# Sliding-window attention and a squared-ReLU FFN in one program: score bursts of three half blocks, one pool of PSUM banks, and another order of the first tasks

## The chip, the cores and the metric

The kernel runs on one core of one Trainium2 chip. The metric is the device time of one execution in microseconds. The engines are named as in the profile: PE is TensorE, PEld its weight loads, DVE is VectorE, ACT is ScalarE, POOL is GpSimd, SP is SyncE. PE writes to PSUM, which has eight banks of 128 rows by 512 fp32 values; ACT and DVE empty them.

## The reference

What is computed, cut to what matters:

```python
# q, k, v: batch 8, 8 heads, 576 tokens, 64 values a head
scores = q @ k.transpose(0, 1, 3, 2) / 8
rel = pos[:, None] - pos[None, :]
slopes = 2.0 ** (-8.0 * (np.arange(8) + 1) / 8)
mask = (rel >= 0) & (rel < 128)
scores = np.where(mask, scores - slopes[:, None, None] * np.abs(rel), -1e9)
attn = softmax(scores)                       # over the keys
x = (attn @ v).transpose(0, 2, 1, 3).reshape(4608, 512)
h = x @ w_in                                 # 512 x 2048
out = (np.maximum(h, 0.0) ** 2) @ w_out      # 2048 x 512, result 4608 x 512 fp32
```

## The kernel before

**Attention.** Each sequence of 576 tokens is cut into blocks of 128, 128, 128, 128 and 64 tokens, 40 blocks in all (`m` counts them, `NKB` is 5). A query block meets at most two key blocks, the previous one (part 0) and its own (part 1). For each block the kernel

- loads k, q and v with a cast to bf16 from POOL's queue (`load_block`, L356). Block 0 alone gets k and q as fp32 by SP's queue (L348);
- transposes k and q to `kqT`: on PE through PSUM (L425, for block 0 L408) with copies on DVE (L373) and ACT (L375) for the blocks in `KQ_PE`, by a DMA transpose on SP's queue (L398) for the others;
- computes scores in a burst (`score`, L469). A contraction over 64 values uses half of the array's rows, so two heads are multiplied side by side, and the two halves write to different PSUM banks. One burst takes four banks for the eight heads. The 64-token last block of a sequence and the first block of the next one share a burst (`pair`);
- exponentiates each bank on ACT into `P` (L488) and multiplies by a mask on DVE (L496), which holds the window and exp(-slope x distance). `masks` are built on ACT (L273) from `dist` (iota on POOL, L245, then DVE); `pair_masks` are copies of them for pair bursts (L280, L283);
- multiplies P with v and a column of ones (`mix`, L516), takes reciprocals (L539) and normalizes (L544) into `x`, which is transposed into `xT` on PE (L562) for the blocks in `X_PE`, or by a DMA transpose on SP's queue (L554).

**FFN.** Tokens go in nine groups of 512. `fc_step` (L604) multiplies w_in with `xT` into a PSUM bank, ACT applies ReLU (L613), DVE squares (L620). `t_part` (L665) multiplies a tile of 128 tokens with w_out, a quarter of the 16 chunks at a time, all into one bank; ACT copies it out (L636) and SP stores it (L644). `SPLIT` cuts the token ranges of the first two groups finer, since their tokens become available bit by bit. w_in and w_out are loaded in four quarters each (L324, L331). `FIRST` gives the order of the first loads on POOL: b is a block (k, q, v), i a quarter of w_in, o one of w_out.

**What sets the order.** Every operation is a `Task` with the engines that it may run on, an assumed duration, a key (its due time) and the slots that it takes and gives back. `Plan.order` walks through time and gives each engine the task that can start first, the smaller key deciding between equals; the program is then emitted in that order, and on the chip each engine runs its instructions strictly in it. Keys come from `where` (blocks, shifted by `AHEAD`) and from the loop over the groups. The planner knows rings of buffers (`size`: 8 slots for k and q, 8 for v, 5 for `kqT`, 2 for `P`, 4 for `x`) and two pools of PSUM banks (`BANKS`): four banks A, used by score bursts and later attention work, and four banks B, used by the FFN and by the first sequence's transposes and PV products. At most eight transfers of a queue are in flight, so a ninth waits for the first to land. `BEGIN` and `COLD` are assumptions on when POOL starts and until when PE runs at half pace. `fill` puts matmuls with zeros (L705, L707; `WARM` of them at the beginning, L311) where the planner sees PE idle before 26 us.

## Time and profile before

| what | value |
|---|---|
| median of 5 runs | 312.88 us (312.34 to 313.34) |
| the profiled execution's own time | 312.67 us |
| its span, first to last instruction | 310.9 us |
| granted clock of TensorE | 1.00 |
| busy: PE, ACT, DVE, POOL | 302.8, 179.2, 164.8, 107.3 us |
| first FFN matmul | 15.92 us |
| last matmul of the FFN ends | 308.0 us |

Times inside the profile count from the span's first instruction. The span is the time of one execution on the chip from the first to the last instruction; what lies around it, 1.8 us here, is in the measured time only. "Busy" for PE is the union of its matmuls' times; they overlap, so the pace of matmuls is read from one start to the next. In lists of groups and in the order in time, `out<-in` names what is written and read, `xN` is a count, and what stands in brackets or behind a bar is the engine's idle time before the group and what ended it. A few per cent of the matmul records can be missing from a trace, and a gap of one matmul's length is then no stall.

### The profile page before, as it was taken

What the parts mean: (1) busy time and instruction counts of PE and PEld (TensorE: products, weight loads), DVE (VectorE), ACT (ScalarE), POOL (GpSimd) and SP (SyncE); (2) the same over time, 40 slices, a digit from 0 to 9 for tenths busy, and PEclk for the clock granted to TensorE, in tenths of its full rate; (3) what the DMA queues carried; (4) which work ended last, traced back from release to release, by engine and by line L of the source; (5) the groups of instructions that cost most, each with busy time, mean ns of one, the idle gap of its engine ahead of it and who ended that gap; (6) DMA issues with size and microseconds to landing.
All of it is one profiled execution on the core that took longest, in us unless ns stands there. A gap on an engine that the chain in (4) does not pass through costs nothing.

```text
span 310.9 us, 7139 instructions
## 1 busy us (share of the span) xinstructions
PE 302.8 (97%) x2784; PEld 173.7 (56%) x2824; DVE 164.8 (53%) x482; ACT 179.2 (58%) x342; POOL 107.3 (35%) x134
## 2 busy tenths in 40 slices
PE   8899999999999999999999999999999999999996
PEld 8799867665455555454454444445444454444443
DVE  5677666566557867675265555556455542222200
ACT  3767748585467847665555656665456654444411
POOL 8936959765654357357432120100000000000100
PEclk9999999999999999999999999999999999999999
DMA  9999999999999999999999994755422120000021
GB/s 136 180 190 180 173 181 131 171 129 142 153 154 145 120 154 163 154 186 172 208 176 161 134 196 118 137 127 104 130 84 84 53 59 34 37 34 35 34 98 73
DMA packets 168114, 39.86 MB, mean 128 GB/s; under 512 B 159440, under 2 KB 163792, under 8 KB 168080
## 3 DMA queue, kind: packets, MB, share of 16 engines
q0 software_dynamic: 114896, 18.88, 87.0%
q1 hardware_dynamic: 53184, 20.52, 34.5%
q8 instruction: 22, 0.36, 0.5%
q14 instruction: 12, 0.10, 0.1%
HBM read 36.70 MB, written 9.44 MB: 148 GB/s over the span
## 4 chain that ended last, share of the span: by engine, by line
PE 95%; ACT 2%; issue 1%; DVE 1%; DVEq 0%
PE B L604 40%; PE B L665 40%; PE A L469 6%; PE A L516 5%; PE A L311 1%; PE B L516 1%; ACT masks L273 1%; PE B L707 1%; ACT kqT L375 1%; PE A L425 1%; PE B L425 0%; DVE kqT L373 0%; PE A L562 0%; PE B L562 0%; ACT P L488 0%
## 5 line engine op out<-in xcount | busy, mean ns | idle before, releaser
L604 PE MATMUL B<-xT,w_in_sb 128*128 128x512 bf16 (+3 forms) x812 | 144.6, 312 | 1.7 <-issue 0.8
L665 PE MATMUL B<-w_out_sb,g 128*128 128x512 bf16 (+2 forms) x572 | 141.5, 373 | 1.3 <-issue 0.5
L613 ACT ACTIVATE rt<-B 128x512 bf16<-128x512 f32 (+2 forms) x152 | 86.6, 584 | 73.4 <-PE B L604 66.1
L620 DVE TENSOR_TENSOR g<-rt 128x512 bf16<-128x512 bf16 (+2 forms) x152 | 61.2, 405 | 73.5 <-ACT rt L613 72.4
L604 PEld LDWEIGHTS <-w_in_sb 128*128 128x128 bf16 x832 | 66.7, 98 | 48.0
L665 PEld LDWEIGHTS <-g 128*128 128x128 bf16 x592 | 54.2, 98 | 55.9
L488 ACT ACTIVATE P<-A 128x512 bf16<-128x512 f32 (+1 forms) x132 | 69.4, 591 | 19.2 <-PE A L469 19.1
L496 DVE TENSOR_TENSOR P<-P,masks 128x512 bf16<-128x512 bf16 (+1 forms) x104 | 42.4, 413 | 25.7 <-ACT P L488 22.3
L356 POOL DMA_DIRECT2D kq<-in_k_dram x39 | 33.0, 847 | 46.5 <-DMA kqT<-kq 34.8
L356 POOL DMA_DIRECT2D vt<-in_v_dram x40 | 34.3, 858 | 39.5 <-PE A L516 33.8
L356 POOL DMA_DIRECT2D kq<-in_q_dram x39 | 33.2, 852 | 11.2 <-DMA vt<-in_v_dram 4.1
L636 ACT ACTIVATE osb<-B 128x512 f32<-128x512 f32 (+1 forms) x36 | 21.6, 600 | 23.9 <-PE B L665 23.9
L516 PEld LDWEIGHTS <-P 128*128 128x128 bf16 x576 | 26.8, 98 | 14.8 <-DVE P L496 0.5
L644 POOL DMA_DIRECT2D out_dram<-osb x3 | 1.7, 563 | 89.5 <-ACT osb L636 89.5
L544 DVE TENSOR_TENSOR x<-A,rec 128x256 bf16<-128x256 f32 (+1 forms) x70 | 28.8, 418 | 1.3
L516 PE MATMUL A<-vt,P 128*128 128x65 bf16 x504 | 25.8, 193 | 0.0
L469 PEld LDWEIGHTS <-kqT 64*128 64x128 bf16 x576 | 14.9, 94 | 13.0 <-issue 12.2
L469 PE MATMUL A<-kqT,kqT 64*128 64x128 bf16 (+1 forms) x256 | 17.9, 212 | 1.0 <-DVE kqT L373 0.8
L469 PE MATMUL A<-kqT 64*128 64x128 bf16 (+1 forms) x320 | 18.4, 211 | 0.0
L539 DVE RECIPROCAL rec<-A 128x4 f32<-128x4 f32 (+1 forms) x70 | 12.1, 179 | 11.7 <-PE A L516 10.8
L496 DVE TENSOR_TENSOR P<-P,pair_masks 128x512 bf16<-128x512 bf16 x28 | 11.7, 420 | 6.7 <-ACT P L488 5.6
L638 DVE COPY osb<-B 128x128 f32<-128x128 f32 x1 | 0.3, 291 | 13.7 <-PE B L665 13.7
(48 smaller groups left out, 80.8 us busy)
## 6 DMA issues: line engine op xcount, KB each, us to landing
out_dram<-osb SPq DMA_DIRECT2D x32, 256.0 KB, 2.3
vt<-in_v_dram POOLq DMA_DIRECT2D x32, 128.0 KB, 7.1
kq<-in_k_dram POOLq DMA_DIRECT2D x31, 128.0 KB, 7.3
kq<-in_q_dram POOLq DMA_DIRECT2D x31, 128.0 KB, 7.7
w_in_sb<-in_moe_w_in_dram POOLq DMA_DIRECT2D x4, 512.0 KB, 9.6
w_out_sb<-in_moe_w_out_dram POOLq DMA_DIRECT2D x4, 512.0 KB, 9.3
out_dram<-osb POOLq DMA_DIRECT2D x3, 256.0 KB, 2.5
kq<-in_k_dram POOLq DMA_DIRECT2D x8, 64.0 KB, 9.4
```

The costliest lines, as they stand in the source:

```text
L356: nc.gpsimd.dma_start(o, src[b, :, kb * 128:kb * 128 + n, :].rearrange("h s d -> s h d"))
L469: nc.tensor.matmul(slot_s[2 * (c // 2) + half].tile.rearrange("p (c x) -> p c x", c=2)[:, c % 2, at:at + w], kqT[sk_of[mk].idx][rows, c, : ...
L488: nc.scalar.activation(Pv(i), view(slot_s[i].tile.rearrange("p (c x) -> p c x", c=2)), AF.Exp, bias=0.0, scale=scale)
L496: nc.vector.tensor_tensor(pt, pt, view(mk), op=ALU.mult)
L516: nc.tensor.matmul(bank(slot_v)[:, hi * (D + 1):(hi + 1) * (D + 1)], Pt[sP.idx][:, place(h)].rearrange("p t q -> p (t q)")[:, at_of[m, par ...
L539: nc.vector.reciprocal(srec.tile[0:n, :], pv[0:n, :, D])
L544: nc.vector.tensor_tensor(xt[sx.idx][0:n, hf * 256:(hf + 1) * 256].rearrange("p (h e) -> p h e", h=4), pv[0:n, :, 0:D], srec.tile[0:n, :]. ...
L604: nc.tensor.matmul(bank(slot)[:, fi * w:(fi + 1) * w], w_in_sb[:, cc, fc * 128:(fc + 1) * 128], xT[:, cc, g * 512 + lo:g * 512 + hi], star ...
L613: nc.scalar.activation(srt.tile[:, 0:cols], slot.tile[:, 0:cols], AF.Relu, bias=0.0, scale=1.0)
L620: nc.vector.tensor_tensor(sg.tile[:, fcs[0]:fcs[-1] + 1, lo:hi], r, r, op=ALU.mult)
L636: nc.scalar.activation(so.tile[:, lo:hi], slot.tile[:, lo:hi], AF.Copy)
L665: nc.tensor.matmul(bank(slot)[:, lo:hi], sg.tile[:, fc, t * 128:(t + 1) * 128], w_out_sb[:, fc, lo:hi], start=fc == 0, stop=fc == FCB - 1)
```

## The change

- Score bursts: `layout` and `score` replace `score`. The four banks of a block's (or a pair's) scores are two units of two banks. From block 5 on, a burst has three units, that is one and a half blocks, in six banks; before that it has two. `P` and `kqT` slots are taken and given back unit by unit.
- PSUM: one pool of eight banks (`BANKS = {"A": 8}`) for everything. `ration` keeps an FFN task from taking a bank when the next burst is near in time and three banks with FFN results are still held.
- First tasks: another `FIRST` order; v of block 0 comes after block 1's k and q (`V0`); iota comes after the first k load; `ident` in bf16 is a task of its own, later; the masks' columns are the other way round (own block first); the pair masks are built after the masking of block 1; `WARM` is 16 instead of 24; other assumed times (`BEGIN`, `COLD`).
- Group 1's tokens are cut in four pieces instead of two (`SPLIT`). In the built program 64 matmuls of 320 columns become 128 of 128 and 64 of 64.
- `KQ_PE`: block 9's k and q are transposed by DMA, block 11's on PE. The rings of k, q and of v have seven slots instead of eight. Other shifts in `AHEAD` and `EARLY`.

The diff, cut to its core:

```diff
-    BEGIN = {"POOL": 1250.0}
-
-    def __init__(self, bufs, pools, cold):
+    BEGIN = {"POOL": 780.0}
+
+    def __init__(self, bufs, pools, cold, share):
         self.tasks = []
         self.bufs = bufs
-        self.pools, self.cold = pools, cold
+        self.pools, self.cold, self.share = pools, cold, share
+        self.bursts = []
...
+    def ration(self, t, at, banks, left, used, free):
+        nxt = next((b for b in self.bursts if b.start is None), None)
+        if nxt is None or left[nxt] or nxt.key >= t.key:
+            return at
+        if nxt.ready > max(at, free["PE"]) + self.share[1]:
+            return at
+        for s in nxt.acq:
+            if s.tag in self.bufs and s.idx is None:
+                u = used[s.tag]
+                if len(u) >= self.bufs[s.tag] and u[-self.bufs[s.tag]].left:
+                    return at
+        mine = [s for s in banks if s is not None and s.ffn]
+        spare = self.share[0] - 1 - sum(1 for s in mine if s.left)
+        if spare < 0:
+            return None
+        ends = sorted((s.freed for s in mine if not s.left), reverse=True)
+        return max(at, ends[spare]) if len(ends) > spare else at
...
                 if s.tag in held:
+                    if s.ffn:
+                        at = self.ration(t, at, held[s.tag], left, used, free)
+                        if at is None:
+                            return None
...
-    FIRST = "b0 b1 b2 i0 i1 i2 b3 i3 o0 b4 b5 o1 b6 b7 o2 o3 b8 b9"
-    SPLIT = {0: [(0, 128), (128, 256), (256, 384), (384, 512)], 1: [(0, 192), (192, 512)]}
-    EARLY = -80
-    AHEAD = {10: -60, 1: 60, 4: 90, 9: -60, 5: -60, 0: -30, 12: 60, 11: 90, 2: 60, 8: 90, 7: 60, 6: 0, 3: -30, 24: 30, 14: 0, 18: 30, 25: 0, 23: 30, 16: -30, 13: 30, 21: 0, 19: -30}
+    FIRST = "b0 b1 i0 b2 i1 b3 i2 o0 b4 i3 b5 o1 b6 o2 b7 o3 b8 b9"
+    SPLIT = {0: [(0, 128), (128, 256), (256, 384), (384, 512)], 1: [(0, 192), (192, 320), (320, 448), (448, 512)]}
+    EARLY = -20
+    AHEAD = {10: -60, 1: 30, 4: 30, 9: -60, 5: 0, 0: 0, 12: 60, 11: 0, 2: 60, 8: 30, 7: 60, 6: 0, 3: 30, 24: -30, 14: -60, 18: 30, 25: 30, 23: 30, 16: -30, 13: 60, 21: 0, 19: 30, 17: 0, 22: 0}
     LEAD = 20
...
-    KQ_PE = [0, 1, 2, 3, 4, 5, 6, 7, 8, 9]
+    KQ_PE = [0, 1, 2, 3, 4, 5, 6, 7, 8, 11]
     X_PE = [0, 1, 2, 3, 4, 5, 7, 8, 12, 17]
-    WARM = 24
+    WARM = 16
     FILL, UNTIL = 0.8, 26e3
-    COLD = 0
-    BANKS = {"A": 4, "B": 4}
+    COLD = 5000
+    QUARTERS = 99
+    V0 = 1
+    SHARE, SOON = 3, 500
+    LONG, UNITS = 5, 3
+    W_IN = [0, 4, 8, 12, 16]
+    PAIR_AFTER, PAIR_KEY = 1, -140
+    BANKS = {"A": 8}
...
-    size = {"kq": 8, "v": 8, "kqT": 5, "P": 2, "x": 4}
+    size = {"kq": 7, "v": 7, "kqT": 5, "P": 2, "x": 4}
...
-        nc.gpsimd.iota(dist, pattern=[[-128, 2], [1, 128]], base=128, channel_multiplier=-1,
+        nc.gpsimd.iota(dist, pattern=[[128, 2], [1, 128]], base=0, channel_multiplier=-1,
                        allow_small_or_imprecise_dtypes=True)
 
-    t_iota = plan.add({"POOL": 360.0}, -9.1e5, build_iota)
+    t_iota = plan.add({"POOL": 360.0}, -9e5 + 1.005, build_iota)
...
-        nc.vector.tensor_single_scalar(ident32, dist[:, 1], 0.0, op=ALU.is_equal)
+        nc.vector.tensor_single_scalar(ident32, dist[:, 0], 0.0, op=ALU.is_equal)
+
+    t_ident = plan.add({"DVE": 480.0}, -9e5 - 1, build_ident, [t_iota])
+
+    def build_ident16():
         nc.vector.tensor_copy(ident, ident32)
 
-    t_ident = plan.add({"DVE": 350.0}, -9e5 - 1, build_ident, [t_iota])
+    t_ident16 = plan.add({"DVE": 230.0}, -9e5 + 1, build_ident16, [t_ident])
...
+    t_pair = [plan.add({"DVE": n}, PAIR_KEY, f, t_mask) for n, f in ((670.0, pair_rest), (960.0, pair_own))]
...
-            t_in[m, nm] = load(key + 0.01 * i, 870.0 * n / 128, emit, deps, [sl])
+            t_in[m, nm] = load(key + 0.01 * i + V0 * (m == 0), 870.0 * n / 128, emit, deps, [sl])
...
+    def layout(ms):
         sP = Slot("P")
-        t_P = []
         pair = len(ms) == 2
-        slot_s = [Slot("A") for _ in range(4)]
         work_of = []
         for i, m in enumerate(ms):
             b, kb, n, _, first = where(m)
             parts_of[m] = ([(0, m - 1)] if kb else []) + [(1, m)]
-            P_of[m] = (sP, t_P)
+            P_of[m] = (sP, [])
             for part, mk in parts_of[m]:
-                at = 128 * i + 64 * part if pair and i == 0 else 128 * part
+                at = 64 * (1 - part) if pair and i == 0 else 128 if pair else 128 * (1 - part)
                 at_of[m, part] = at
                 rel = [sk_of[mk]] if part == 0 or kb == NKB - 1 else []
                 work_of.append((m, mk, n, at, rel))
-        lo = min(w[3] for w in work_of)
-        hi = max(w[3] + w[2] for w in work_of)
-        n = 128 if pair else work_of[0][2]
+        for m in ms:
+            P_of[m] = P_of[ms[0]]
+        return ms, sP, work_of, where(ms[0])[3]
+
+    def score(units):
+        first_of = [u for u in units if u[1] == 0]
+        due = units[0][0][3]
+        slots = {}
+        for (ms, sP, work_of, _), j in units:
+            for half in range(2):
+                slots[ms[0], 2 * j + half] = Slot("A")
 
         def burst():
-
-            for sl in slot_s:
+            for sl in slots.values():
                 bank(sl)
-            for c in range(C):
-                for m, mk, w, at, _ in work_of:
-                    for half in range(2):
-                        rows = slice(half * 64, half * 64 + 64)
-                        nc.tensor.matmul(
-                            slot_s[2 * (c // 2) + half].tile.rearrange("p (c x) -> p c x", c=2)[
-                                :, c % 2, at:at + w],
-                            kqT[sk_of[mk].idx][rows, c, :], kqT[sk_of[m].idx][rows, C + c, 0:w],
-                            start=True, stop=True)
-        tm = plan.add({"PE": 220.0 + C * sum(max(w[2], 64) / 2.4 + 4 for w in work_of)}, due - 28, burst,
-                      [t for w in work_of for x in w[:2] for t in t_kq_of[x]] + chain["s"], slot_s + [sP],
-                      [x for w in work_of for x in w[4]])
+            for (ms, sP, work_of, _), j in units:
+                for c in (2 * j, 2 * j + 1):
+                    for m, mk, w, at, _ in work_of:
+                        for half in range(2):
+                            rows = slice(half * 64, half * 64 + 64)
+                            nc.tensor.matmul(
+                                slots[ms[0], 2 * j + half].tile.rearrange("p (c x) -> p c x", c=2)[:, c % 2, at:at + w],
+                                kqT[sk_of[mk].idx][rows, c, :], kqT[sk_of[m].idx][rows, C + c, 0:w],
+                                start=True, stop=True)
+        tm = plan.add({"PE": 220.0 + 2 * sum(max(w[2], 64) / 2.4 + 4 for u in units for w in u[0][2])}, due - 28, burst,
+                      [t for u in units for w in u[0][2] for x in w[:2] for t in t_kq_of[x]] + chain["s"],
+                      [*slots.values()] + [u[0][1] for u in first_of],
+                      [x for u in units if u[1] == 1 for w in u[0][2] for x in w[4]])
+        plan.bursts.append(tm)
         chain["s"] = [tm]
-        for i in range(4):
-            def view(t):
+        for (ms, sP, work_of, due), j in units:
+            pair = len(ms) == 2
+            hi = max(w[3] for w in work_of) // 128 + 1
+            lo = min(w[3] for w in work_of) // 128
+            n = 128 if pair else work_of[0][2]
+            cols = 2 * sum(w[2] for w in work_of)
+
+            def view(t, pair=pair, lo=lo, hi=hi, n=n):
                 if pair:
                     return t
-                return t.rearrange("p c (t q) -> p c t q", t=2)[:, :, lo // 128:2, 0:n]
-
-            def Pv(i=i):
-                return view(Pt[sP.idx][:, 2 * i:2 * i + 2].rearrange("p h t q -> p h (t q)"))
-
-            def expo(i=i):
-                nc.scalar.activation(Pv(i), view(slot_s[i].tile.rearrange("p (c x) -> p c x", c=2)),
-                                     AF.Exp, bias=0.0, scale=scale)
-            cols = 2 * sum(w[2] for w in work_of)
-            te = plan.add({"ACT": act(cols)}, due - 28 + 3 * i, expo, [tm], [], [slot_s[i]])
-
-            def mask(i=i):
-                pt = Pv(i)
-                mk = (pair_masks if pair else masks.rearrange("p h t q -> p h (t q)"))[:, 2 * i:2 * i + 2]
-                nc.vector.tensor_tensor(pt, pt, view(mk), op=ALU.mult)
-            t_P.append(plan.add({"DVE": dve(cols, 2)}, due - 28 + 3 * i, mask,
-                                [te] + (t_pair if pair else [t_mask[h] for h in range(H) if place(h) // 2 == i])))
+                return t.rearrange("p c (t q) -> p c t q", t=2)[:, :, lo:hi, 0:n]
+
+            for i in (2 * j, 2 * j + 1):
+                slot = slots[ms[0], i]
+
+                def Pv(i=i, sP=sP, view=view):
+                    return view(Pt[sP.idx][:, 2 * i:2 * i + 2].rearrange("p h t q -> p h (t q)"))
+
+                def expo(i=i, Pv=Pv, view=view, slot=slot):
+                    nc.scalar.activation(Pv(i), view(slot.tile.rearrange("p (c x) -> p c x", c=2)),
+                                         AF.Exp, bias=0.0, scale=scale)
+                te = plan.add({"ACT": act(cols)}, due - 28 + 3 * i, expo, [tm], [], [slot])
+
+                def mask(i=i, pair=pair, Pv=Pv, view=view):
+                    pt = Pv(i)
+                    mk = (pair_masks if pair else masks.rearrange("p h t q -> p h (t q)"))[:, 2 * i:2 * i + 2]
+                    nc.vector.tensor_tensor(pt, pt, view(mk), op=ALU.mult)
+                P_of[ms[0]][1].append(plan.add(
+                    {"DVE": dve(cols, 2)}, due - 28 + 3 * i, mask,
+                    [te] + (t_pair if pair else [t_mask[h] for h in range(H) if place(h) // 2 == i])))
...
+    units, ready = [], []
     while m < NBLK:
         ms = [m, m + 1] if m % NKB == NKB - 1 and m + 1 < NBLK else [m]
         for x in ms:
             turn(x)
-        score(ms)
-        for x in ms:
-            mix(x)
+        what = layout(ms)
         m += len(ms)
+        for j in range(2):
+            units.append((what, j))
+            if j:
+                ready.append(ms)
+            if len(units) < (UNITS if ms[0] >= LONG else 2) and not (m >= NBLK and j):
+                continue
+            score(units)
+            units = []
+            for done_ms in ready:
+                if done_ms[0] == PAIR_AFTER:
+                    for t in t_pair:
+                        t.deps += P_of[done_ms[0]][1]
+                for x in done_ms:
+                    mix(x)
+            ready = []
...
-        slot = Slot("B")
+        slot = Slot("A")
+        slot.ffn = True
...
```

Other places change `Slot("B")` to `Slot("A")`, set `slot.ffn` for the FFN, and let `SPLIT` pieces wait for their own quarter of w_in.

## The prediction

> **What bounds the kernel now.** I read the page first (busy shares, the chain that ended last), then the order in time on TensorE (PE) and on the other engines for the first 45 us, then the landings of the transfers, last the waits.
>
> The page:
>
> ```profile
> span 310.9 us, 7139 instructions
> PE 302.8 (97%) x2784; PEld 173.7 (56%) x2824; DVE 164.8 (53%) x482; ACT 179.2 (58%) x342; POOL 107.3 (35%) x134
> ...
> PE 95%; ACT 2%; issue 1%; DVE 1%; DVEq 0%
> ```
>
> PE is the bound: 95% of the chain. A busy PE need not be at its peak, so I took the distance from each matmul's start to the next. From the first FFN matmul (15.92) on, every one runs at its form's own pace: 216 ns for 512 columns, 136 for 320, 83 for 192, 56 for 128, 29 for 65. Gaps of one matmul too many are missing records (2784 matmuls against 2824 weight loads: 40). Real stalls are 0.21 us at 24.1, 0.11 at 33.7, 0.09 at 52.1, and none after. So later only the amount of PE work and the cost of changing kinds of work can move the end.
>
> A score burst in the order in time (start, length, engine, line, tiles, count), its middle left out:
>
> ```profile
> 104.17 1.46 PE L604 MATMUL B<-xT,w_in_sb 128*128 128x512 bf16 x6
> 105.56 0.23 PE L469 MATMUL A<-kqT,kqT 64*128 64x128 bf16 x2
> ...
> 105.96 0.22 PE L469 MATMUL A<-kqT 64*128 64x128 bf16 x2
> 106.11 0.39 PE L665 MATMUL B<-w_out_sb,g 128*128 128x512 bf16 x1
> ```
>
> The last of the six starts at 104.17 + 5 x 0.216 = 105.25, the burst 0.31 later instead of 0.216: 95 ns to go over to 64-row matmuls. From the last pair's second matmul to the next full one are 149 ns instead of 53: 96 ns to come back. A burst costs 0.19 us besides its pairs (57 ns each at 128 columns), whatever its length.
>
> The start:
>
> ```profile
> 6.48 0.60 PE L408 MATMUL B<-ident,kq 128*128 128x128 f32 x4
> ...
> 15.92 1.05 PE L604 MATMUL B<-xT,w_in_sb 128*128 128x128 bf16 x16
> ...
> 7.12 0.69 DVE L373 CAST kqT<-B 128x512 bf16<-128x512 f32 x1 [2.07 <-PE B L408]
> ...
> 6.67 2.55 ACT L273 ACTIVATE masks<-dist 128x256 bf16<-128x256 f32 x8
> 9.12 1.18 ACT L488 ACTIVATE P<-A 128x256 bf16<-128x256 f32 x4
> ```
>
> ACT builds the eight masks after its copy of kqT, and exp waits for it. This sets the 15.92. Two issues of loads on POOL, and from the answers for them alone the time to landing (min/median/max):
>
> ```profile
> 12.57 0.80 POOL L324 DMA_DIRECT2D w_in_sb<-in_moe_w_in_dram  x1
> ...
> 20.16 0.68 POOL L356 DMA_DIRECT2D vt<-in_v_dram  x1 [2.11 <-DVE x L544]
> ```
>
> ```profile
> DMA to landing us min/median/max: 6.9/9.6/12.2
> ```
>
> ```profile
> DMA to landing us min/median/max: 9.2/9.2/9.2
> ```
>
> The last quarter of w_in lands at 12.57 + 12.2 = 24.8 and is first read at 26.1; v of block 4 lands at 29.3. The loads land in order, one 128-row block per 0.85 us, one weight quarter per 2.5, without a pause from 12 us: in the first 45 us a load's place in the queue decides its time. Before, the least margin between landing and use there is 1.0 us.
>
> **The change, part by part.**
> *Bursts.* Before: 33 (26 single blocks, 7 pairs). After: 5 of blocks 0 to 5, then 56 half units in threes, 19; 24 in all. Nine times 0.191 = -1.72 us; pairs and columns stay. The Trainium skill (TensorEngine Tiling, Key Properties) says that a change of tiling mode drains TensorE, and TensorE: Matmul & The Clock Gate (Single matmul latency) puts a drain near 175 ns: an estimate of 2 x 175 x 9 = 3.15 us. The rows show 95 and 96 ns; I take 1.72.
> *Group 1's split.* 64 matmuls of 320 columns become 128 of 128 and 64 of 64: 128 x 56 + 64 x 29 (the 65-column pace) - 64 x 136 = +0.32 us.
> *One pool, FFN held.* No operation. A long burst takes six banks and leaves two. The Trainium skill speaks against it (TensorEngine Tiling, Gotcha 1: row tiling raises PSUM pressure; Perfetto Trace Analysis, Optimization Strategy: a bubble that recurs can mean that PSUM ran out). By the rows: exp frees a bank every 0.48 us (four in 2.06), the first 0.8 after the burst; an FFN step of four matmuls fills one per 0.86, a tile of the second GEMM one per 3.5. The two free banks carry PE 1.7 us, by when two exps are done; with a relu (0.49) per step, ACT needs 0.97 against PE's 0.86 for six steps, 0.7 us behind at most, inside that lead. Bounds are that and 0; I take 0; without cover, ACT's lag, up to 0.7, falls on PE at each of 19 bursts. In the new order I counted PE work between each bank's last write and its reuse against ACT's and DVE's queues: least slack after 55 us 0.15 us (before: over 0.3). The same count names before's stalls at 24.1, 33.7 and 52.1.
> *The start.* POOL issues block 1's k and q first (0.86 each), iota between them, then v0, v1 and w_in's first quarter. Iota ends 1 us later, but ident waits for DVE's memsets anyway (to 2.2). Both fp32 copies go to DVE (0.69 each; 7.8 as now). ACT starts the masks at 4.7, when dist is ready, and ends them at 7.1 instead of 9.2. Block 1's q is the fourth transfer instead of the fifth (8.0 before, about 7.2), so its transposes stand ahead of burst 0 at no cost. Burst 1 goes from 11.3 to 8.7; eight exps end at 11.6; mask, norm, four transposes and copy of x follow: first FFN near 13.5, -2.4. The pair masks (0.34 + 0.53 on DVE) move behind block 1's masks, into that chain only ahead of x1.
> *What that meets.* w_in's third quarter now comes after block 3: the same loads as had landed with v3 before (11.70 + 11.1 = 22.8). The fourth comes after w_out's first and block 4: those that had landed with v4 (29.3). I take 0.2 off each for the earlier first issue. PE's work from first FFN to the third quarter: 79 x 56 + 16 x 29 + 16 transposes and 9 fillers x 56 + two bursts (1.3) = 7.6 us plus 0.4 of stalls by my count: there at 21.5, waits to 22.6. Thence 6.5 us more (85 x 56, 3 x 216, 16 x 29, 12 x 56): 29.1; the fourth quarter's landing says 29.2. Of 2.4 us won, some 1.5 go back. What is late next is w_out's second (before 33.7, same place; needed near 35.9): covered.
> *Behind this gate.* From 26.1 to its last matmul at 308.0, PE takes 281.9 us before. After, behind the same first use, by counts: FFN in +100 x 56 + 64 x 29 - 64 x 136 = -1.24; FFN out -3 x 216 = -0.65; 16 PV x 29 = -0.46; 12 transposes x 56 = -0.67; 9 bursts -1.72; a filler -0.06. Sum -4.8: 277.1.
> *Block 9's transpose to DMA, block 11's to PE; rings of 8 to 7; new due times.* PE and ACT work equal. On SP block 9's transpose now stands with block 10's ahead of x of block 6: nothing if that x is written later than both issue, which by order it is. A load has six blocks (some 37 us) of lead against 14.6 at most to land. Three x transposes have 8.6, 9.05 and 9.07 us from issue to use; rows of that stage:
>
> ```profile
> L554 SPq DMA_TRANSPOSE xT<-x x5: 1208/1317/2212, 78.6 to 105.1; - x5
> ...
> DMA to landing us min/median/max: 7.6/8.4/9.2
> ```
>
> They land 0.6 us late to 1.5 early (before, the tightest had 8.64 and 1.05 us to spare). A kqT has 10.7 against 7.6 to 12.1. Bounds 0 to 2 us; taken 0, as before's closest did not stall.
> *Sum.* 29.2 + 277.1 = 306.3 against 308.0; the tail of copy and store (2.9 us) stays. 312.67 - 1.7 = 311.0 for the profiled execution; the median is 0.2 above it: **311.2 us**.
>
> **The rivals.**
> 1. *No gate at the weights.* Loads come 1.2 us sooner than I place them; PE reaches the fourth quarter at 13.5 + 14.1 + 0.4 = 28.0. Then -2.9: 310.0. For it: q3 took 1.44 us instead of 0.85 before, which need not recur. Against: the queue never rests.
> 2. *Late transposes.* One or two x or kqT transposes between 60 and 112 us stop PE by 0.5 to 2 us in all: 311.7 to 313.2. For it: the distances above. Against: the tightest before still had a margin, and smaller rings put fewer loads in front.
> 3. *Bank waits: slower.* PE waits on ACT in or after each of the 19 long bursts. It decides at (1.7 + 0.6) / 19 = 0.12 us each; at 0.25 the time is 311.2 + 4.8 = 316.0, at 0.15 314.0. For it: slacks of 0.15. Against: ACT is 58% busy and banks return faster than FFN takes them.
> That the bursts do not get longer is excluded: the built order has 24.
>
> **How the numbers follow.** Mine 0.50 (310.6 to 311.9), rival 1 0.20, rival 2 0.17, rival 3 0.13. Range 309.8 to 312.9: rival 1 whole, rival 2 nearly, rival 3 out. The measurement tells 0.2% (0.63 us) from no change: faster than 312.25, mine and 1 nearly whole and a third of 2: 0.74; same 0.13 (most of rival 2); slower 0.13 (rival 3).
>
> **What would show it.** Right: 24 bursts at 95 and 96 ns; masks done by 7.5; first FFN at 13 to 14; a stall of some 1 us at w_in's third quarter near 22; no later stall over 0.3. Wrong: waits of PE on ACT at the ends of bursts (rival 3), on xT or kqT (2), none near 22 (1), or a first FFN later than 15.

## The result, and the profile after

The changed kernel takes 311.85 us (median of 26 runs, 311.0 to 313.46) against 312.88 us of the kernel before (47 runs): ratio 0.9974, 95% interval 0.9965 to 0.9982. The forecast was 311.2 us. The direction and the range held, the size did not: of 1.7 us forecast, 1.0 us came by the medians and 0.8 us by the means, which the ratio compares. In 3 of the 26 runs (312.98 to 313.46 us) the mean granted clock was 0.995 instead of 0.999 or more, a clock that no run of the kernel before has on record, and without them the gain is 1.0 us by the means too. The profiled execution took 312.47 us.

The page of the changed kernel:

```profile
span 310.7 us, 7356 instructions
PE 301.9 (97%) x2905; PEld 177.5 (57%) x2945; DVE 161.2 (52%) x475; ACT 179.1 (58%) x336; POOL 107.5 (35%) x134
...
PE 89%; DMA 7%; POOL 2%; issue 1%; DVE 0%; POOLq 0%
```

PE is still the bound, but the chain that ended last now leads through transfers: DMA has 7% of it.

A long burst in the order in time on PE (start, length, engine, line, tiles, count), its middle left out:

```profile
103.94 0.38 PE L729 MATMUL A<-w_out_sb,g 128*128 128x512 bf16 x1
104.25 0.23 PE L507 MATMUL A<-kqT,kqT 64*128 64x128 bf16 x2
...
104.88 0.22 PE L507 MATMUL A<-kqT 64*128 64x128 bf16 x2
105.03 1.04 PE L667 MATMUL A<-xT,w_in_sb 128*128 128x512 bf16 x3
```

The burst starts 0.31 us behind the matmul ahead of it, and the next full matmul 0.15 us behind the last pair: 95 and 96 ns over, as before. There are 24 such bursts instead of 33.

The start, ACT:

```profile
5.12 2.56 ACT L306 ACTIVATE masks<-dist 128x256 bf16<-128x256 f32 x8 [3.10 <-DVE dist L294]
8.91 0.60 ACT L407 ACTIVATE kqT<-A 128x512 bf16<-128x512 bf16 x1 [1.22 <-DVE kqT L405]
9.40 3.17 ACT L536 ACTIVATE P<-A 128x256 bf16<-128x256 f32 x8
13.87 0.60 ACT L407 ACTIVATE xT<-A 128x512 bf16<-128x512 bf16 x1 [1.30 <-PE A L610]
```

DVE's two fp32 copies to kqT:

```profile
6.89 1.47 DVE L405 CAST kqT<-A 128x512 bf16<-128x512 f32 x2 [1.44 <-PE A L440]
```

and PE, with the wait ahead of a group and its releaser in brackets:

```profile
5.87 0.97 PE L440 MATMUL A<-ident,kq 128*128 128x128 f32 x4
7.02 0.61 PE L440 MATMUL A<-ident,kq 128*128 128x128 f32 x4
...
8.51 0.40 PE L507 MATMUL A<-kqT 64*128 64x128 bf16 x8
...
13.45 0.39 PE L610 MATMUL A<-ident,x 128*128 128x128 bf16 x4
13.67 0.33 PE L770 MATMUL A<-ident,zero 128*128 128x128 bf16 x3
14.22 0.40 PE L458 MATMUL A<-ident,kq 128*128 128x128 bf16 x4 [0.22 <-DMA kq<-in_k_dram]
15.28 0.40 PE L458 MATMUL A<-ident,kq 128*128 128x128 bf16 x4 [0.66 <-DMA kq<-in_q_dram]
15.51 0.39 PE L772 MATMUL A<-zero 128*128 128x128 bf16 x4
15.73 0.44 PE L667 MATMUL A<-xT,w_in_sb 128*128 128x128 bf16 x5
```

The masks end at 7.68 instead of 9.2. But the exps do not follow them: ACT stands idle for 1.22 us until DVE has written kqT, makes a copy of its own, and starts the exps at 9.40, later than the 9.12 of the kernel before. x of block 0 is transposed at 13.45 and copied by 14.47. Then the transposes of block 2's k and q stand ahead of the first FFN matmul on PE, and they wait for their loads. The first FFN matmul starts at 15.73, against 15.92 before and 13.5 in the forecast. In the kernel before, the same transposes of block 2 waited for nothing:

```profile
12.34 0.61 PE L425 MATMUL B<-ident,kq 128*128 128x128 bf16 x8
```

Those loads on POOL (block 2's k and q), and from the answer for the two alone the time from issue to landing:

```profile
6.10 0.93 POOL L388 DMA_DIRECT2D kq<-in_k_dram  x1
6.97 0.93 POOL L388 DMA_DIRECT2D kq<-in_q_dram  x1
```

```profile
DMA to landing us min/median/max: 8.1/8.2/8.3
```

They land at 14.2 and 15.2, behind w_in's first quarter. Before, ahead of that quarter in the queue, they landed at 9.7 and 10.6.

The waits of PE from 10 to 35 us, and below them those from 36 us to the end (us in total, times, longest):

```profile
PE A L458 <- DMA kq<-in_q_dram: 0.7, 1, 0.7
PE A L667 <- DMA w_in_sb<-in_moe_w_in_dram: 0.4, 1, 0.4
PE A L507 <- DVE kqT L405: 0.3, 1, 0.3
PE A L458 <- DMA kq<-in_k_dram: 0.2, 1, 0.2
```

```profile
PE A L729 <- issue: 0.6, 4, 0.2
PE A L667 <- issue: 0.5, 3, 0.2
```

All waits lie in the first 35 us. Those called "issue" are gaps of one 512-column matmul, that is, records that the trace lacks. No engine and no transpose holds PE later.

### The profile page after: what moved, and what is told of

It is laid out like the page before. It is cut to its first block, busy times and chain, and to the rows that moved or that the text cites. A ratio compares the mean times of both kernels' runs of the same rounds, so it can differ in the third digit from the quotient of the medians.

```text
span 310.7 us, 7356 instructions
## 1 busy us (share of the span) xinstructions
PE 301.9 (97%) x2905; PEld 177.5 (57%) x2945; DVE 161.2 (52%) x475; ACT 179.1 (58%) x336; POOL 107.5 (35%) x134
## 4 chain that ended last, share of the span: by engine, by line
PE 89%; DMA 7%; POOL 2%; issue 1%; DVE 0%; POOLq 0%
PE A L729 40%; PE A L667 38%; PE A L564 5%; PE A L507 5%; DMA kq<-in_q_dram 4%; DMA vt<-in_v_dram 3%; POOL kq L388 1%; PE A L458 1%; PE A L610 1%; POOL vt L388 1%; POOL w_in_sb L357 0%; POOL dist L274 0%; DVE osb L701 0%; POOLq L274 0%; POOLq L808 0%
## 5 line engine op out<-in xcount | busy, mean ns | idle before, releaser
L667 PE MATMUL A<-xT,w_in_sb 128*128 128x512 bf16 (+3 forms) x944 | 147.9, 293 | 1.6 <-issue 0.5
L729 PE MATMUL A<-w_out_sb,g 128*128 128x512 bf16 (+2 forms) x568 | 143.5, 373 | 1.7 <-issue 0.6
L676 ACT ACTIVATE rt<-A 128x512 bf16<-128x512 f32 (+1 forms) x146 | 85.4, 600 | 73.7 <-PE A L667 59.1
L683 DVE TENSOR_TENSOR g<-rt 128x512 bf16<-128x512 bf16 (+1 forms) x146 | 61.0, 418 | 84.6 <-ACT rt L676 83.7
L667 PEld LDWEIGHTS <-w_in_sb 128*128 128x128 bf16 x960 | 70.9, 98 | 48.2 <-DMA w_in_sb<-in_moe_w_in_dram 0.6
L543 DVE TENSOR_TENSOR P<-P,masks 128x512 bf16<-128x512 bf16 (+1 forms) x104 | 42.4, 411 | 19.9 <-ACT P L536 16.4
L388 POOL DMA_DIRECT2D kq<-in_q_dram x39 | 33.4, 856 | 13.6 <-DMA kq<-in_k_dram 5.8
L699 ACT ACTIVATE osb<-A 128x512 f32<-128x512 f32 (+1 forms) x36 | 21.7, 602 | 22.2 <-PE A L729 21.2
L564 PEld LDWEIGHTS <-P 128*128 128x128 bf16 x576 | 26.3, 98 | 12.7
L592 DVE TENSOR_TENSOR x<-A,rec 128x256 bf16<-128x256 f32 (+1 forms) x80 | 32.3, 414 | 0.6
L564 PE MATMUL A<-vt,P 128*128 128x65 bf16 x576 | 29.2, 193 | 0.0
L587 DVE RECIPROCAL rec<-A 128x4 f32<-128x4 f32 (+1 forms) x80 | 13.6, 176 | 9.5 <-PE A L564 8.2
L543 DVE TENSOR_TENSOR P<-P,pair_masks 128x512 bf16<-128x512 bf16 x28 | 11.6, 419 | 3.3 <-ACT P L536 2.6
L407 ACT ACTIVATE kqT<-A 128x512 bf16<-128x512 bf16 (+1 forms) x9 | 5.2, 580 | 8.5 <-DVE kqT L405 5.8
## 6 DMA issues: line engine op xcount, KB each, us to landing
w_in_sb<-in_moe_w_in_dram POOLq DMA_DIRECT2D x4, 512.0 KB, 10.4
```

Of the source, the lines that this page charges most:

```text
L388: nc.gpsimd.dma_start(o, src[b, :, kb * 128:kb * 128 + n, :].rearrange("h s d -> s h d"))
L543: nc.vector.tensor_tensor(pt, pt, view(mk), op=ALU.mult)
L564: nc.tensor.matmul(bank(slot_v)[:, hi * (D + 1):(hi + 1) * (D + 1)], Pt[sP.idx][:, place(h)].rearrange("p t q -> p (t q)")[:, at_of[m, par ...
L587: nc.vector.reciprocal(srec.tile[0:n, :], pv[0:n, :, D])
L592: nc.vector.tensor_tensor(xt[sx.idx][0:n, hf * 256:(hf + 1) * 256].rearrange("p (h e) -> p h e", h=4), pv[0:n, :, 0:D], srec.tile[0:n, :]. ...
L667: nc.tensor.matmul(bank(slot)[:, fi * w:(fi + 1) * w], w_in_sb[:, cc, fc * 128:(fc + 1) * 128], xT[:, cc, g * 512 + lo:g * 512 + hi], star ...
```

## How the runs are compared

Two times describe each profiled execution: F, the start of the first FFN matmul, and E, the start of PE's last matmul. The whole time is 4.8 to 4.9 us above E in every kernel (312.67 and 307.81 before, 312.47 and 307.61 after). E - F, less the waits of PE that lie between the two, is the PE work; F and those waits tell what the start and the loads do. A ratio below is the mean time of a kernel over the mean time of the kernel before on the same chip; times from different chips differ by some tenths of a us, so that kernels are compared by their ratios.

| kernel | block 2's q lands | F | E | E - F |
|---|---|---|---|---|
| before, three profiles | 10.6, 10.4, 11.3 | 15.92, 16.05, 15.77 | 307.81, 308.08, 307.65 | 291.9, 292.0, 291.9 |
| changed, three profiles | 15.2, 14.6, 15.1 | 15.73, 15.13, 15.59 | 307.61, 307.22, 306.65 | 291.9, 292.1, 291.1 |
| w_in's first quarter behind block 2 | 10.8 | 15.43 | 306.19 | 290.8 |
| before, quarter ahead of block 2 | 14.4 | 18.66 | 310.55 | 291.9 |
| PE's block 2 behind the FFN | 16.3 | 14.69 | 307.83 | 293.1 |
| pause ahead of the quarter, twice | 14.6, 14.5 | 15.09, 14.98 | 306.36, 306.05 | 291.3, 291.1 |
| first quarter in halves | 13.0 | 15.14 | 305.96 | 290.8 |
| halves, block 2's k and q first, twice | 11.1, 11.0 | 14.32, 14.22 | 305.67, 306.30 | 291.4, 292.1 |
| long bursts up to block 19 | 14.9 | 15.35 | 307.86 | 292.5 |
| the load order of before in the changed kernel | 11.9 | 16.47 | 310.01 | 293.5 |
| pause behind the quarter | 14.9 | 15.43 | 307.54 | 292.1 |
| halves with the pause | 13.5 | 15.67 | 307.21 | 291.5 |

## The experiments

**The place of w_in's first quarter.** My first reading was a dry transfer queue: the quarter is the fifth load on POOL now, and the four block loads ahead of it are too few to cover its slow start. Two kernels move only this load on POOL. Four kernels ran on one chip, the changed kernel among them.

> The changed kernel once more, beside the kernel before on the same chip. All theories: 0.2 to 0.4% faster, some 311.9 us; first FFN matmul near 15.7 us, w_in's third quarter landing near 24.5 and its fourth near 30.8.

Measured: 311.73 us, ratio 0.9961 (0.9947 to 0.9976).

```diff
+    done.remove(t_win[0])
+    done.insert(done.index(t_in[2, "v"]) + 1, t_win[0])
```

> The changed kernel with one move on POOL: w_in's first quarter is issued after block 2's three loads instead of ahead of them; no other engine's order changes. Theory (the transfer queue runs nearly dry behind the fifth load, because a weight quarter takes 2 to 4 us from its issue to full rate and four block loads are too few to cover that): every load from block 2's on lands about 1.8 us sooner, k and q of block 2 near 10 us, the third quarter near 22.5, the fourth near 29.2; the first FFN matmul starts near 13.5 to 14.5 unless the first quarter itself is then late; time about 310.3, 0.5% below the changed kernel. Rival (a first weight quarter is slow wherever it stands, so that the loss belongs to the quarter and not to its place): the third and fourth quarters still land near 24.5 and 30.8, time 311.8.

Measured: 311.33 us, ratio 0.9960 (0.9944 to 0.9976), not told apart from the changed kernel. Block 2's q landed at 10.8, but the quarter only at 15.4, and the first FFN matmul waited for it: F 15.43. The third quarter landed at 23.0 and the fourth at 29.8, against 23.6 and 30.3 beside it. The wait for block 2 (0.3 to 1.1 us in the three profiles of the changed kernel) was exchanged for one of 1.0 us for the quarter; PE met none behind it. The expectation named this only as an exception.

In the kernel before, the same move the other way:

```diff
+    done.remove(t_win[0])
+    done.insert(done.index(t_in[1, "v"]) + 1, t_win[0])
```

> The kernel before with one move on POOL: w_in's first quarter is issued after block 1's three loads instead of after block 2's, fifth in the queue as in the changed kernel; no other engine's order changes. Theory of the dry queue: loads from block 2's on land 1 to 2 us later than in the kernel before, w_in's fourth quarter near 26 instead of 24.8; the least margin was 1.0 us there, so PE stops for up to 1 us: 312.9 to 313.9. Rival (the quarter is slow wherever it stands): later loads land as before within 0.3 us and the time is 312.9.

Measured: 315.42 us, ratio 1.0072 (1.0051 to 1.0094). The loads behind block 2 landed within the spread of the kernel before (fourth quarter 25.5), as the rival said. The time went to what both had overlooked: block 2's k landed at 13.6 instead of 9.7, PE waited 2.0 us for it and 0.4 us for q, and then ran at half clock for 3.4 us (see the last section). F rose by 2.7, E - F stayed at 291.9.

Two more profiles of the kernel before:

> The kernel before once more, for a second look at its landings. Theory (up to block 2's v the loads land 4.6 to 5.0 us behind their issue, one per issue on POOL, and only from w_in's first quarter on does the transfer itself set the pace): again 4.6 to 5.0 us for every load up to block 2's v, the first quarter at 14.3 to 14.9, third 19.5 to 20.0, fourth 24.6 to 25.1, block 4's v 29.2 to 29.7. If the landings of single looks differ by 1 us, the lateness seen in the changed kernel may be chance.

Measured: 312.98 us; the first quarter came later than the expected 14.3 to 14.9. Its landing, issued at 7.6, from the answer for this load alone:

```profile
L324 POOL DMA_DIRECT2D w_in_sb<-in_moe_w_in_dram x1: 817/817/817, 7.6 to 7.6; - x1
...
DMA to landing us min/median/max: 8.4/8.4/8.4
```

It landed at 16.0, the fourth quarter at 26.2: both 1.4 us later than in the profile that the forecast was made from, with E only 0.3 later.

> A third look at the landings of the kernel before. The two looks so far have w_in's first quarter at 14.55 and 16.00 us, its fourth at 24.77 and 26.17. Theory (the first weight load takes 3.5 to 3.9 us from the load before it, and 2.8 in the first look was the exception): again 3.5 us or more, first quarter at 15.3 or later, fourth at 25.5 or later, and a time that hardly follows it (312.5 to 313.1), since the kernel before has 1.0 us to spare there. Rival (2.8 is usual, and the changed kernel's order makes the loss): 14.8 or earlier and 25.1 or earlier.

Measured: 312.57 us; quarters at 14.8 and 25.0. So the answer lies between. As the eighth load on POOL the first quarter landed 2.8, 3.7 and 2.3 us behind the load ahead of it in the kernel before, and 3.6 and 3.5 us in two variants of the changed kernel (the one with the quarter behind block 2, and the next one below). As the fifth, with no pause ahead, it took 3.7 to 5.0 us in eight profiles, 4.0 on the mean, and 2.7 in the profile of the changed kernel shown above, where v of block 1 itself came late, at 10.7. The fifth place costs some 0.5 to 1 us there, and single profiles scatter by as much.

**The whole load order of before in the changed kernel**

```diff
-    FIRST = "b0 b1 i0 b2 i1 b3 i2 o0 b4 i3 b5 o1 b6 o2 b7 o3 b8 b9"
+    FIRST = "b0 b1 b2 i0 i1 i2 b3 i3 o0 b4 b5 o1 b6 b7 o2 o3 b8 b9"
-    V0 = 1
+    V0 = 0
```

> The changed kernel with the load order of before (block 2 ahead of w_in, w_in's quarters together, v of block 0 at its old place), the rest kept and planned anew; 24 bursts as in the changed kernel. Theory (bursts give 1.7, group 1's split takes 0.3, and the new load order gains nothing because the fifth load leaves the queue short): 311.3 to 311.9, no more than 0.3 from the changed kernel. Rival (the new load order does give what was forecast for the start): 312.2 or more. Third way (it even costs): 310.9 or less. Fourth quarter near 25.1, first FFN matmul 14.8 to 15.5.

Measured: 314.16 us, ratio 1.0031 (1.0015 to 1.0047). My 311.3 to 311.9 was wrong. The first quarter landed at 16.4, F was 16.47, and PE waited 0.4 and 0.5 us for w_in's second and third quarters and 0.3 for a q at 56 us. With the rest of this plan the new load order is worth some 2 us (0.57% by the ratios); that it gains nothing is refuted. The plan around it was made anew and its due times were not.

**The bursts.** Three kernels go back to one block or pair a burst, from block 5, 14 or 20 on:

```diff
-    LONG, UNITS = 5, 3
+    LONG, UNITS = 5, 2
```

> The changed kernel without the long bursts: every burst is one block or pair (33 instead of 24), the rest of the change kept and planned anew. Theory (a burst costs 0.19 us, six banks held cost nothing): 9 x 0.191 = 1.7 us more than the changed kernel, 313.6. Rival (bank waits after long bursts eat part of the gain): less than 1 us more, 312.0 to 312.8, or none.

```diff
-            if len(units) < (UNITS if ms[0] >= LONG else 2) and not (m >= NBLK and j):
+            if len(units) < (UNITS if LONG <= ms[0] < 14 else 2) and not (m >= NBLK and j):
```

> The changed kernel with long bursts only up to block 13; from block 14 on a burst is one block or pair again: 31 bursts instead of 24, the start untouched. Theory (0.19 us for each burst, bank waits nothing): 7 x 0.191 = 1.3 us slower than the changed kernel, 313.0 to 313.3. Rival (the long bursts' gain is partly eaten by waits): 0.3 to 0.8 us slower, 312.1 to 312.6.

Measured: 317.13 us, ratio 1.0139 (1.0104 to 1.0174), and 318.19 us, ratio 1.0174 (1.0148 to 1.0199): 3.5 and 5 us more than the theory gave. The planner's new order issues transposes by DMA too late. From the waits of PE behind 36 us, first of the kernel with short bursts from block 14, then of the one from block 5:

```profile
PE A L667 <- DMA xT<-x: 2.8, 1, 2.8
```

```profile
PE A L507 <- DMA kqT<-kq: 3.0, 3, 2.1
```

In the first of the two the xT in question was issued at 106.76 and landed 7.6 us later, no slower than the 7.2 to 9.6 of the changed kernel, but PE wanted it at 111.9. This is what the second rival of the forecast described, in a neighbour of the kernel. For the bursts these two runs say nothing; block 20 lies behind that stretch:

```diff
-            if len(units) < (UNITS if ms[0] >= LONG else 2) and not (m >= NBLK and j):
+            if len(units) < (UNITS if LONG <= ms[0] < 20 else 2) and not (m >= NBLK and j):
```

> The changed kernel with long bursts up to block 19 and single blocks or pairs from block 20 on: 29 bursts instead of 24. The order of all work up to about 165 us is that of the changed kernel, so that the stretch from 60 to 115 us, where the kernels with short bursts from block 5 and from block 14 stopped for transposes by DMA, is untouched. Theory (0.19 us for each burst, bank waits nothing): 5 x 0.191 = 0.95 us above the changed kernel, 312.8, with no stall of PE after 35 us. Rival (long bursts' gain partly eaten by waits for banks): 0.2 to 0.6 us above. Third way (any new order brings late transposes): 2 us or more above, with the stall to be seen.

Measured: 313.04 us, ratio 1.0004 (0.9989 to 1.0018) against 0.9974 of the changed kernel: 0.30% or 0.94 us for five bursts, with no wait behind 36 us. The two intervals leave some 0.5 us either way, but E - F less waits says the same: 292.05 against 290.8 to 291.4. 0.19 us for a burst holds.

**The early wait or the row of loads?** One kernel delays the loads, one takes the early wait away on PE alone. In the first, POOL does three more iotas ahead of the quarter:

```diff
         for t in done:
+            if t is t_win[0]:
+                for _ in range(3):
+                    nc.gpsimd.iota(idle, pattern=[[128, 2], [1, 128]], base=0, channel_multiplier=-1,
+                                   allow_small_or_imprecise_dtypes=True)
             t.emit()
```

> The changed kernel with three more iotas into an unused tile on POOL, 1.0 us in all, ahead of w_in's first quarter; the order of all else as it was. Theory (the landings of block 2's k and q and of w_in's quarters set the end one for one): every load from w_in's first quarter on lands 0.8 to 1.0 us later and the time rises by as much, to 312.6 to 312.8; if the longer wait at block 2's k lowers the granted clock, as in the kernel before with its first quarter moved ahead, up to 1.5 more. Rival (PE is not held by the landings, the missing gain lies elsewhere): 311.6 to 312.0.

Measured: 311.30 us, ratio 0.9945 (0.9932 to 0.9959). Wrong in sign: the quarter, issued 1.2 us later, landed at 12.0 instead of the 12.7 to 13.6 of the eight profiles with the same order of loads and no pause ahead. So the run was repeated with the changed kernel and two variants on one chip.

> The changed kernel once more, on the chip of its variants: 311.7 to 311.9 by all theories, first FFN 15.1 to 15.7, stalls at w_in's third quarter and block 4's q of 0.5 to 1.2 us in all.

Measured: 312.05 us, ratio 0.9987 (0.9970 to 1.0003), 0.15 us above the expected range.

> The three iotas ahead of w_in's first quarter once more. If the 311.30 of the first time is real: again 0.3 to 0.6 us below the changed kernel, with the first quarter landing near 12 us although issued 1.2 us later, and block 2's q and all later loads no later than in the changed kernel. If it was chance: 311.7 or more.

Measured: 311.18 us, ratio 0.9955 (0.9939 to 0.9971). The gain came twice: 0.29% and 0.32% by the ratios, against the changed kernel's first runs and against those beside it. POOL in that kernel, the landing of the quarter, and what the transfers moved in single microseconds (busy times of PE, PEld, DVE, ACT and POOL with their counts, then clock, transfer share and GB/s):

```profile
5.37 1.24 POOL L796 IOTA idle<- 128x256 f32 x3
6.55 0.77 POOL L358 DMA_DIRECT2D w_in_sb<-in_moe_w_in_dram  x1
```

```profile
DMA to landing us min/median/max: 5.5/5.5/5.5
```

```profile
8.00:9.00 1.00, 0.68 (x18) 0.60 (x18) 0.06 (x2) 0.96 (x3) 1.00 (x2) 1.00 0.73 40
9.00:10.00 1.00, 1.00 (x28) 0.90 (x23) 1.00 (x5) 1.00 (x4) 1.00 (x3) 1.00 1.13 185
10.00:11.00 1.00, 1.00 (x22) 0.97 (x20) 0.89 (x5) 1.00 (x3) 1.00 (x2) 1.00 1.22 197
```

The same for the changed kernel beside it:

```profile
8.00:9.00 1.00, 0.94 (x18) 0.65 (x15) 0.49 (x2) 0.39 (x1) 1.00 (x2) 1.00 1.11 133
9.00:10.00 1.00, 0.74 (x20) 0.63 (x20) 0.48 (x2) 1.00 (x5) 1.00 (x2) 1.00 1.06 158
10.00:11.00 1.00, 1.00 (x24) 0.98 (x22) 0.90 (x5) 1.00 (x4) 1.00 (x2) 1.00 1.27 185
```

With the pause the transfers nearly stop at 8 to 9 us and the quarter then starts at once at 185 GB/s; without it, it comes to 185 only at 10 to 11 us. A dry queue costs nothing here, so my first theory falls. To see which neighbours slow the quarter, the pause went behind it:

```diff
-            if t is t_win[0]:
+            if t is t_in[2, "k"]:
```

> The changed kernel with the three iotas (1.0 us) behind w_in's first quarter and ahead of block 2's k on POOL. Theory A (the quarter is slowed by the loads that are issued behind it while it runs): it lands near 11 us, 5.5 behind its issue at 5.35, block 2's q near 14.5 to 14.8, time 311.0 to 311.4. Theory B (the quarter is slowed by the four block loads ahead of it, and a pause there lets them drain): it lands at 12.7 to 13.3 as in the changed kernel, block 2's q at 14.7 to 15.5 or later, time 311.7 to 312.1.

Measured: 311.91 us, ratio 0.9976 (0.9963 to 0.9989); the quarter landed at 13.2, block 2's q at 14.9. This is theory B: it is what stands ahead of the quarter that matters, not what follows. Why block loads in front slow it is not settled.

Now the early wait, taken away by the order of tasks (indices into the emitted list):

```diff
+    part = done[117:168]
+    turn_2 = [part[i - 117] for i in (117, 118, 120, 121, 122, 123, 124, 125, 126, 128, 132)]
+    burst_2 = [part[i - 117] for i in (145, 153, 163)]
+    rest = [t for t in part if t not in turn_2 + burst_2]
+    cut = rest.index(done[157])
+    done[117:168] = rest[:cut] + turn_2 + rest[cut:] + burst_2
```

> The changed kernel with block 2's eight transposes, their two copies and its burst moved behind the first 16 to 26 FFN matmuls on PE, ACT and DVE; the loads are as they were. The first FFN matmul then waits only for x and w_in's first quarter and starts near 14.0 instead of 15.1 to 15.7 us. Theory (the wait for block 2's q is where the forecast start failed, and the end follows it): up to 1.1 us less than the changed kernel, 310.7 to 311.2, with small stalls later. Rival (the landings of w_in's third quarter near 23.5, block 4's q near 27.5 and the fourth quarter near 30 hold PE anyway): the stalls there grow by what is won before, and the time stays within 0.4 us of the changed kernel, 311.4 to 311.9.

Measured: 312.10 us, ratio 0.9976 (0.9962 to 0.9990), level with the 312.05 beside it. F came to 14.69, but:

```profile
14.69 0.44 PE L667 MATMUL A<-xT,w_in_sb 128*128 128x128 bf16 x5 [0.46 <-ACT xT L407]
...
19.74 0.90 PE L667 MATMUL A<-xT,w_in_sb 128*128 128x128 bf16 x13 [0.76 <-DMA w_in_sb<-in_moe_w_in_dram]
```

What is won at block 2's q is lost again: 0.76 us at w_in's second quarter (landed at 19.7 in this profile, where all loads from the first quarter on were late; 18.0 to 18.6 in the three of the changed kernel), and 0.59 us at block 2's own burst, for a kqT that the move made late. The median of 12 runs, which does not hang on one profile, shows no gain either. So the time is as the rival said: taking away this one wait gains nothing. That the row of loads sets the pace is what this profile and the swap suggest; the second wait of 0.59 us is a cost of the move itself and has nothing to do with loads.

**Smaller first pieces.** So a version must move the loads. The first quarter in two halves, the second behind block 2:

```diff
-    FIRST = "b0 b1 i0 b2 i1 b3 i2 o0 b4 i3 b5 o1 b6 o2 b7 o3 b8 b9"
+    FIRST = "b0 b1 i0 b2 i1 i2 b3 i3 o0 b4 i4 b5 o1 b6 o2 b7 o3 b8 b9"
-    W_IN = [0, 4, 8, 12, 16]
+    W_IN = [0, 2, 4, 8, 12, 16]
```

> The changed kernel with w_in's first quarter loaded in two halves, the second one behind block 2. Theory (a weight load costs by its bytes plus some 1 us that it takes to come to full rate): the first half lands near 11.5, k and q of block 2 near 12.5 and 13.3, so that PE gets to its first FFN matmul near 14 instead of 15.5, while w_in's last piece still lands near 30 and holds PE there: 311.3 to 311.8. Rival (the slow start takes 3.6 us whatever the size): block 2's q lands at 14.3 or later and nothing moves: 311.8.

Measured: 310.88 us, ratio 0.9944 (0.9923 to 0.9966). The half landed at 11.3, block 2's k and q at 12.2 and 13.0, the last piece at 29.4: the landings as expected. The time was somewhat better than expected with F at 15.14 and not near 14: PE's order there has block 2's burst ahead of the first FFN matmul, and PE met no wait behind it. With block 2's k and q ahead of the half besides:

```diff
+    done.remove(t_win[0])
+    done.insert(done.index(t_in[2, "q"]) + 1, t_win[0])
```

> The kernel with w_in's first quarter in halves, with block 2's k and q issued ahead of the first half, v behind it; only POOL's order differs. Theory (the first weight load costs its 1.25 us plus 1 us wherever it stands): k and q of block 2 land near 10 and 10.8 instead of 12.2 and 13.0, the first half near 13 to 13.5; the stall of 0.57 us at block 2's q goes, the first FFN matmul starts 0 to 0.5 us sooner; later loads as in the kernel with halves, so that part of it comes back at block 4's q: 310.4 to 310.9. Rival (the first half itself is late then and holds the first FFN): 311 or more.

Measured: 311.00 us, ratio 0.9930 (0.9916 to 0.9943), F 14.32: 0.1 us above what was expected, with F 0.8 us sooner.

> Halves of the first quarter, block 2's k and q ahead of them, once more: 310.6 to 311.2, 0.6 to 1.2 below the changed kernel beside it, first FFN matmul near 14.3 behind burst 2, stalls of some 0.4 us at w_in's second half and 0.3 at block 4's q.

Measured: 311.28 us, ratio 0.9952 (0.9935 to 0.9970), again 0.1 us above what was expected, against 312.05 of the changed kernel on that chip. Both versions beat the kernel before; against the changed kernel the second is clear in its first trial (0.9930 against 0.9974), while the interval of the first version just touches the changed kernel's. Between the two nothing is decided. The halves with the pause ahead of the first:

> The kernel with w_in's first quarter in halves and block 2 behind the first half, with the same pause of 1.0 us ahead of the first half. If the pause gains there as it did with the whole quarter: the first half lands near 11 although issued 1.2 us later, block 2's q near 12.9, and 310.3 to 310.8. If the small first piece has already taken that gain: the first half lands at 11.9 to 12.5, block 2's q near 13.6 to 14, and 310.9 to 311.6.

Measured: 311.98 us, ratio 0.9982 (0.9969 to 0.9995); half at 11.8, q at 13.5. This is above both ranges. The pause gains nothing ahead of the small piece; that it costs rests on a comparison across chips (0.9944 without it).

## Why the prediction was right in direction and wrong in size

- *Bursts, -1.72:* right. 24 bursts, 95 and 96 ns, and five of them undone cost 0.94 for 0.95.
- *Group 1's split, and behind the gate:* right. E - F less waits went from 291.9 to between 290.8 and 291.4. The forecast's 306.3 counts to the end of the last matmul, 306.1 to its start; less 13.5 and 1.5 of waits that is 291.1. What PE does ahead of F is not quite the same in both kernels, and stalls of 0.1 to 0.3 us inside a group are not in the list of waits, so tenths are not told apart.
- *One pool, FFN held, 0:* right. PE waits for neither ACT nor DVE behind 36 us; the third rival is out.
- *Transposes moved to and from DMA, 0:* right for this kernel, and by luck of its due times as much as by the margins: in two neighbours PE stopped for 2.8 and 3.0 us for them.
- *The start:* **this step failed**, in two places that cost about 1 us each. First, "exp waits for it", the masks, was true before and no longer after. The masks did come sooner (7.7; 7.1 forecast), but now the exps waited for the copies of kqT. Both fp32 copies on DVE end at 8.36 and not "7.8 as now", burst 0 starts at 8.51, and ACT's copy of block 1's kqT stands ahead of the exps, so that they end at 12.6, 12.7 and 12.3 in the three profiles instead of 11.6. With x's transposes and copy behind them the first FFN matmul could have started at 14.5, 14.6 and 14.2, and not at 13.5. The kernel with block 2 behind the FFN shows it: exps until 12.74, F 14.69, with PE waiting for ACT's copy of xT. Second, block 2's k and q, whose loads the change moves behind w_in's first quarter, were not followed at all, though their transposes stand ahead of that matmul on PE. By the forecast's own rates q would have landed at 9.0 + 2.5 + 2 x 0.85 = 13.2, which costs 0.2 us; it landed at 14.6 to 15.2, and F came at 15.1 to 15.7. Why it landed so late is the next step.
- *What that meets* took a quarter at 2.5 us "without a pause". **This term was mis-sized:** as fifth load the first quarter landed 3.7 us or more behind the load ahead of it in eight of nine profiles. The third quarter came at 23.4 to 24.5 instead of 22.6, the fourth at 29.9 to 30.8 instead of 29.2: 1.2 and 1.1 us late on the mean. Part of that is the draw of the one profile that the forecast was made from: the same places in the queue landed at 22.8 and 29.3 there, at 23.1 and 29.9 on the mean of three profiles of the kernel before. The rest, 0.9 and 0.6 us, is left for the new order. The waits there were 0 to 0.4 us, not 1.1, since PE came later, and 0 to 0.4 at block 4's q, which was not foreseen.
- *Sum:* mean F of three profiles 15.5 instead of 13.5, +2.0; mean E - F 291.7 instead of 292.6, -0.9; E +1.1, as much as their mean time of 312.0 lies above the 311.0 forecast for a profiled execution; the median is 0.65 above its forecast. The gain at the start did not go to an engine later on but into two waits that the forecast had not looked for, one for copies of kqT and one for loads.
- *What would show it wrong* named "a first FFN later than 15". That is what came; and of the stall of some 1 us at w_in's third quarter "near 22", which was to show it right, one profile of three has 0.4 us, at 24.5.

## What to carry to other kernels

When what an instruction waits for is made to come sooner, ask what it will wait for next: here the masks came 1.5 us sooner and the exps behind them not at all. When a load is moved, follow every load that it now stands in front of to its first reader, and every instruction queued ahead of the work that is to come sooner. Landing times from one profile are one draw: in the kernel before they scattered by 1.4 us while E moved by 0.4. Taking one wait away on the waiting engine moved it to the next load; moving the loads themselves, with smaller first pieces, gained.

## What the runs showed of the hardware

First, a long wait costs PE twice. The kernel with long bursts up to block 13 waits 2.8 us at 111.9; the columns of these stretches are busy times, then PEclk, transfer share and GB/s:

```profile
111.00:114.60 3.60, 0.86 (x4) 0.20 (x2) 1.24 (x4) 0.27 (x1) 2.45 (x3) 1.00 1.77 160
114.60:116.00 1.40, 1.36 (x11) 0.82 (x12) 0.08 (x1) 0.00 (x0) 0.88 (x1) 0.60 1.84 90
116.00:118.00 2.00, 2.00 (x29) 1.14 (x28) 0.95 (x3) 1.18 (x3) 0.00 (x0) 0.50 1.69 151
118.00:120.00 2.00, 1.95 (x13) 0.98 (x12) 1.67 (x6) 1.59 (x4) 1.39 (x3) 0.92 2.43 155
```

In finer stretches the granted clock is 0.5 from 114.9 to 118.3 us, that is for 3.4 us, which costs up to 1.7 us more. The same came with a wait of 2.1 us in the kernel with short bursts from block 5 (108.5 to 111.9) and with the waits of 2.0 and 0.4 us in the kernel before with its quarter moved ahead (14.0 to 17.4). One such stretch makes the mean clock of an execution 0.995. A wait of 1.44 us in the kernel with short bursts from block 5 left the clock at 1.00:

```profile
13.50:15.20 1.70, 0.26 (x6) 0.09 (x3) 0.75 (x4) 0.60 (x1) 0.72 (x1) 1.00 1.74 181
15.20:16.00 0.80, 0.80 (x15) 0.80 (x16) 0.00 (x0) 0.15 (x1) 0.57 (x1) 1.00 1.32 204
```

The Trainium skill (TensorE: Matmul & The Clock Gate, What's actually happening) lets the clock fall after an idle window of about 3.4 us; here waits of 2.0 to 2.8 us were enough, so that the measured wait is the figure to plan with.

Second, PE starts at half pace, and for how long differs from one execution to the next. In the profile of the changed kernel the fillers before 5.8 us start every 0.11 us, those behind 6.6 us every 0.056; the four fp32 transposes that begin at 5.87 take 0.97 us, those at 7.02 take 0.61. The last filler at half pace starts between 3.6 and 6.8 us in the twenty profiles. In the changed kernel and its variants (but for the one with the load order of before) the masks always end at 7.7, but the exps start at 8.5 to 8.8 in the four where half pace ends before 5 us, and at 9.5 to 9.6 in the two where it lasts to 6.7 or 6.8. So part of the scatter of F comes from PE and not from the loads. In the kernel before the masks, done at 9.0 to 9.2, hid it. What sets the moment no run here shows.

Third, 1.2 us of pause ahead of a large load made it land sooner (12.0 instead of 12.7 to 13.6) and the kernel 0.3% faster, twice.
